# Batch 1's Z from float16 halves, and all steps from the first conversions on in another order

## The chip, the cores and the metric

One core of one Trainium2 chip runs the kernel. The core has TensorE (PE) for matrix products, VectorE (DVE), ScalarE (ACT) and GpSimd (POOL) for the rest, SyncE (SP) whose queue issues every transfer here, and 16 DMA engines. The metric is the device time of one execution in microseconds, as the median of three.

## The reference, cut to what matters

```python
def sm_attn(qq, kk, vv):
    s = scale * np.matmul(qq, kk.transpose(0, 1, 3, 2))
    s = s - np.max(s, axis=-1, keepdims=True)
    a = np.exp(s)
    a = a / (np.sum(a, axis=-1, keepdims=True) + 1e-09)
    return np.matmul(a, vv)
p_packed = sm_attn(p, k, v)                # 32 packed rows per head
out = sm_attn(q, p_packed, p_packed)       # 576 rows per head
...
h = x @ w_in                               # x: (4608, 512), w_in: (512, 1024)
sm = e / (np.sum(e, axis=-1, keepdims=True) + 1e-09)   # e = exp(h - max h)
solu = h * sm
ln = (solu - mu) / np.sqrt(var + 1e-06) * g_ln
return ln @ w_out                          # (1024, 512)
```

There are 8 batches of 8 heads, 576 rows and 64 columns per head, all float32; the weights come as float64.

## The kernel before, in words

The second attention's values are the 32 packed rows, so the kernel multiplies these by `w_in` first. For each batch b it makes Z = packed rows times `w_in` (4 heads of 32 rows side by side, 1024 columns, two groups r), and a row's h is then its attention weights a times Z. Weights a and Z are each kept as a float16 high part and a float16 low part, and a product is three float16 products.

Work per batch, each a generator whose `yield`s cut it into steps:

- `pack(b)` (steps `k0` to `k7`): k transposed (for batches 0 and 1 by PE, line 369, else by DVE, line 383), scores of the packed rows (line 399), their maximum `nmx` (DVE, 403) and exp (ACT, 406), the exps transposed by PE (422) and copied to `e1T` (424), the product with v (432), its scaling `pp` (DVE, 435), the transposed packed rows `ppT` (448), and a size (320).
- `unpack(b)` (`q0` to `q7`): q transposed, scores (504 or 516), brought back in blocks by DVE (477), maximum `mx` (481), subtraction (483), exp (486), sum (489), reciprocal (494), scaling (496), DVE's transposition (527), high part `a_h` (ACT, 530) and low part `a_l` (532).
- `make_z(b)` (`z0` to `z7`): with `ZP_BY[b]` '0' 16 float32 products of the packed rows with `w_in_sb` (570); with '1' 48 float16 products (564) of the packed rows' halves `pph` (551, 553) with the halves of `w_in`. Those halves are made by `weight_halves` (steps `H`): four times `w_hi` on ACT (342) and the low part on DVE (344), 128 by 1024 each. Z itself is split into halves by ACT and DVE (578, 580).
- `token_tile` (`t0` to `t35`, 128 rows each; every fifth one takes its rows from two batches): 12 products h = a Z (631), row maximum `nm` (DVE, 634), its scaled form and exp (ACT, 639, 652), `u` = e times h (DVE, 656), float16 halves `yhl` of u minus its mean (ACT 665, DVE 667), a transposing DMA to `yT` (670), sum of squares (ACT, 673), a row factor on POOL (676 to 683), 24 products with `w_out`'s halves `wch` and `wcl` (691) into PSUM `po` or `h`, scaling to `o_sb` (697, 699) and the DMA out (708).
- Once: the conversion of float64 weights to float32 (steps `W0` to `W3`, `O0` to `O3`: ACT 229, DVE 231, POOL or ACT 240/242, POOL 263 or 271, DVE 250), `w_out`'s halves (`C0` to `C7`, lines 305 to 313), p's transposition (`p`, 209), loads (`lp`, `lw`, `lo`, `lk`, `lq`, `lv`). Steps `Z` (lines 117, 119) and `X` (125) are products that nothing reads, made to keep PE's clock up.

Nothing schedules this at run time: the string `ORDER` of 1287 names says which generator takes its next step, and each engine runs its instructions in the order in which they are issued so. Short strings say which engine takes a step: `LOW_BY`, `PT_BY`, `KT_BY`, `QT_BY`, `E1T_BY`, `SOFT_BY`, `A2L_BY`, `SCALED_BY` ('a' ACT, 'd' DVE, 'p' or 'g' POOL).

PSUM has three two-bank tiles `h`, shared by token tiles, transposes, scores and Z, one `po` and one `pa`. A float32 tile of raw k, q or `w_out` has three buffers; `e`, `u`, `yhl` and `yT` have two each. The four `w_out` conversions work in place in the buffers of `yT` and `yhl`.

## Time and profile before

| | us |
|---|---|
| median of 3 runs | 389.76 |
| lowest and highest | 389.49, 390.90 |
| the profiled execution | 390.44 |
| its span, first to last instruction | 388.6 |
| PE busy in the span | 373.8 |
| DVE busy | 294.3 |
| ACT busy | 256.7 |
| POOL busy | 244.8 |

The profiled execution's time is 1.8 us over its span and 0.7 us over the median. The span falls into three parts. Until 54 us the weights, p, k, q and v of batch 0 arrive and are converted, and the first weights a and the first Z are made. From 54 to 364 us PE works through the products of the token tiles, with the pieces of the next batches between them. The last 21 us are the last four tiles' products with `w_out`. Rows of a timeline name an engine's work in order of time, with the idle time before it in square brackets and what ended that.

### The profile page before, as it was taken

How to read it: one execution, taken by the hardware profiler on the slowest of the kernel's cores; microseconds unless marked ns; L12 is line 12 of the kernel's file. 1: busy time of each engine (PE TensorE's matmuls, PEld its weight loads, DVE VectorE, ACT ScalarE, POOL GpSimd, SP SyncE). 2: the span in 40 equal slices, each digit the busy share in tenths (PEclk: the TensorE clock that was granted, in tenths of full speed). 3: DMA queues.
4: the chain of work that ended last, by engine and by line, in shares of the span. 5: the costliest groups of instructions: out<-in, count | busy, mean ns of one | idle time of the engine just before them, and what ended most of it. 6: DMA issues, size and time to landing. Idle time of an engine off the chain costs nothing.

```text
span 388.6 us, 8528 instructions
## 1 busy us (share of the span) xinstructions
PE 373.8 (96%) x3234; PEld 190.9 (49%) x3234; DVE 294.3 (76%) x472; ACT 256.7 (66%) x447; POOL 244.8 (63%) x410
## 2 busy tenths in 40 slices
PE   6978979999999999999999999999999999999996
PEld 6856435444545444544454455444444444444444
DVE  2577888999987987778798589977777968466631
ACT  2566799795878678955767657754658559465730
POOL 2674689887438987764555476875456658854550
PEclk9989999999999999999999999999999999999999
DMA  8999894898899999999697878873632435353561
GB/s 310 385 375 355 195 213 89 201 167 183 150 228 166 201 215 172 175 180 230 143 199 145 204 142 189 189 167 67 128 81 59 107 108 83 83 132 86 83 162 54
DMA packets 213017, 66.10 MB, mean 170 GB/s; under 512 B 192872, under 2 KB 206960, under 8 KB 212464
## 3 DMA queue, kind: packets, MB, share of 16 engines
q1 hardware_dynamic: 212976, 65.56, 74.4%
q8 instruction: 25, 0.41, 0.5%
q14 instruction: 16, 0.13, 0.1%
HBM read 37.23 MB, written 9.44 MB: 120 GB/s over the span
## 4 chain that ended last, share of the span: by engine, by line
PE 71%; DVE 4%; DMA 2%; ACT 1%; POOL 1%; issue 1%; SPq 0%; DVEq 0%; ACTq 0%
PE po L691 37%; PE h L631 19%; PE h L691 5%; PE h L564 2%; PE pa L432 2%; PE h L399 2%; PE h L516 1%; DMA yT<-yhl 1%; PE h L422 1%; DMA raw<-in_q_dram 1%; DVE u L656 1%; DVE w_in_sb L344 1%; DVE nm L634 1%; ACT e L652 1%; DVE s L477 0%
## 5 line engine op out<-in xcount | busy, mean ns | idle before, releaser
L691 PE MATMUL po<-wch,yT 128*128 128x512 f16 x512 | 160.1, 379 | 0.1
L691 PEld LDWEIGHTS <-yT 128*128 128x128 f16 x888 | 85.8, 98 | 100.6 <-issue 5.3
L691 PE MATMUL po<-wcl,yT 128*128 128x512 f16 x256 | 97.0, 379 | 0.0
L656 DVE SCALAR_TENSOR_TENSOR u<-e,s_row,h 128x1024 f32<-128x1024 f32 x36 | 45.8, 1271 | 18.3 <-ACT e L652 12.9
L667 DVE SCALAR_TENSOR_TENSOR yhl<-u,negmu,yhl 128x1024 f16<-128x1024 f32 x36 | 47.5, 1319 | 4.7 <-ACT yhl L665 4.6
L634 DVE TENSOR_REDUCE nm<-h 128x1 f32<-128x1024 f32 x36 | 43.5, 1212 | 8.3 <-PE h L631 7.9
L631 PE MATMUL h<-zh,a_h 128*128 128x512 f16 (+2 forms) x168 | 47.7, 380 | 0.7 <-ACT qT L371 0.7
L631 PE MATMUL h<-zl,a_h 128*128 128x512 f16 (+2 forms) x168 | 47.9, 380 | 0.0
L631 PEld LDWEIGHTS <-a_h 128*128 128x128 f16 (+2 forms) x336 | 27.7, 100 | 34.6 <-issue 5.2
L652 ACT ACTIVATE e<-h,nmc,z_scale 128x1024 f32<-128x1024 f32 x36 | 43.2, 1201 | 1.9 <-PE h L631 0.8
L665 ACT ACTIVATE yhl<-u,negmu 128x1024 f16<-128x1024 f32 x36 | 41.1, 1145 | 0.7
L673 ACT ACTIVATE e<-u,negmu 128x1024 f32<-128x1024 f32 x36 | 40.9, 1137 | 0.0
L639 ACT ACTIVATE nmc<-nm,z_scale 128x1 f32<-128x1 f32 x33 | 9.6, 292 | 45.9 <-DVE nm L634 45.9
L642 POOL TENSOR_SCALAR bound<-nm,z_scale 128x1 f32<-128x1 f32 x33 | 12.9, 390 | 37.6 <-DVE nm L634 36.1
L680 POOL TENSOR_SCALAR c_row<-sq,s_eps 128x1 f32<-128x1 f32 x36 | 12.8, 355 | 29.3 <-ACT e L673 26.4
L631 PE MATMUL h<-zh,a_l 128*128 128x512 f16 (+2 forms) x84 | 30.4, 379 | 0.1
L631 PE MATMUL h<-zl,a_l 128*128 128x512 f16 (+2 forms) x84 | 30.4, 379 | 0.0
L699 DVE TENSOR_SCALAR o_sb<-po,c_row,inv 128x512 f32<-128x512 f32 x18 | 14.6, 810 | 13.8 <-PE po L691 6.9
L681 POOL TENSOR_TENSOR c_row<-c_row,neg_half 128x1 f32<-128x1 f32 x36 | 22.5, 626 | 3.0
L660 ACT ACTIVATE negmu<-su 128x1 f32<-128x1 f32 x36 | 7.2, 200 | 25.5 <-DVE u L656 25.4
L496 POOL TENSOR_TENSOR a<-a,sm 128x576 f32<-128x576 f32 x16 | 20.3, 1274 | 4.9 <-DVE sm L494 4.3
L532 POOL TENSOR_TENSOR a_l<-s,a_h 128x576 f16<-128x576 f32 x14 | 20.4, 1460 | 4.5 <-ACT a_h L530 4.5
(173 smaller groups left out, 687.8 us busy)
## 6 DMA issues: line engine op xcount, KB each, us to landing
out_dram<-o_sb SPq DMA_DIRECT2D x34, 256.0 KB, 2.3
v_sb<-in_v_dram SPq DMA_DIRECT2D x8, 1024.0 KB, 8.3
raw<-in_k_dram SPq DMA_DIRECT2D x24, 288.0 KB, 4.4
raw<-in_q_dram SPq DMA_DIRECT2D x96, 72.0 KB, 2.5
zh<-in_moe_w_in_dram SPq DMA_DIRECT2D x2, 1024.0 KB, 8.0
zl<-in_moe_w_in_dram SPq DMA_DIRECT2D x2, 1024.0 KB, 7.9
raw<-in_k_dram SPq DMA_DIRECT2D x2, 1024.0 KB, 12.2
raw<-in_moe_w_out_dram SPq DMA_DIRECT2D x2, 1024.0 KB, 8.4
```

What stands on the lines that cost most here:

```text
L496: EN(nc, SOFT_BY[2 * b + 1]).tensor_tensor(out=w2, in0=w2, in1=sm.unsqueeze(2).broadcast_to([P, NB, J]), op=ALU.mult)
L532: EN(nc, A2L_BY[2 * b + r]).tensor_tensor(out=lo, in0=a2T, in1=hi, op=ALU.subtract)
L631: nc.tensor.matmul(dst_[:, cols], lhsT=lhsT, rhs=z[:, r, cols], start=bool(first), stop=bool(last))
L634: nc.vector.tensor_reduce(out=nm, in_=h, axis=AX.X, op=ALU.max, negate=True)
L652: nc.scalar.activation(e, h, AF.Exp, bias=nmc, scale=sc[:, 1:], accum_out=se)
L656: nc.vector.scalar_tensor_tensor(out=u, in0=e, scalar=s_row, in1=h, op0=ALU.mult, op1=ALU.mult, accum_out=su)
L665: nc.scalar.activation(yhl[:, 0], u, AF.Identity, bias=negmu)
L667: nc.vector.scalar_tensor_tensor(out=yhl[:, 1], in0=u, scalar=negmu, in1=yhl[:, 0], op0=ALU.add, op1=ALU.subtract)
L673: nc.scalar.activation(e, u, AF.Square, bias=negmu, accum_out=sq)
L681: nc.gpsimd.tensor_tensor(out=c_row, in0=c_row, in1=neg_half, op=ALU.pow)
L691: nc.tensor.matmul(po[:, cols], lhsT=yT[:, a, c], rhs=w[:, c, cols], start=c == 0 and t == 0, stop=c == NFC - 1 and t == 2)
L699: nc.vector.tensor_scalar(out=o_sb[:, cols], in0=po[:, cols], scalar1=c_row, scalar2=inv, op0=ALU.mult, op1=ALU.mult)
```

## The change

`ZP_BY[1]` becomes '1': batch 1's Z is made like those of batches 2 to 7, by 48 float16 products in place of 16 float32 ones, and the four pairs of `weight_halves` come before it (`H` steps moved forward). `warm_up` is cut into eleven steps: six of four float32 products, five of three wide ones. `SOFT_BY` gets an entry for each r and each of the two operations, `E1T_BY` entries for all batches, and `weight_halves` a branch for POOL that no entry takes (`HL_BY` is 'dddd'). `ORDER` is another string from its eleventh name on. Line numbers after the change are larger by 1 in the upper part of the code, by 4 from `keep_clock` on and by 8 from `z_scale` on.

```diff
-SCALED_BY = 'gggggggg'
+SCALED_BY = 'ggggggdg'
-A2L_BY = 'ddpppppppppppppp'
-SOFT_BY = 'ppppppppdppppppp'
-LOW_BY = 'appapaaa'
+A2L_BY = 'pdppppdpdpppppdp'
+SOFT_BY = 'pppppppppdppppppppdpdpppdppdpdpd'
+LOW_BY = 'aaapaaap'
-PT_BY = 'aaaa'
-KT_BY = 'ddaaaaaaaaaaaaa'
-QT_BY = 'dadaaaaaaaaaaaa'
-E1T_BY = 'aaaaaa'
+PT_BY = 'ddda'
+KT_BY = 'ddaadaaaaaaaaaa'
+QT_BY = 'dadadaaaaaaaaaa'
+E1T_BY = 'ddadaaaadddaaaaa'
-ZP_BY = '00111111'
+ZP_BY = '01111111'
+HL_BY = 'dddd'
...
     def warm_up():
-        for _ in range(24):
-            nc.tensor.matmul(spare[:, :P], lhsT=ones_f, rhs=ones_f, start=True, stop=True)
-        for _ in range(15):
-            nc.tensor.matmul(spare, lhsT=ones, rhs=ones.unsqueeze(1).broadcast_to([P, DM // P, P]), start=True, stop=True)
-        yield
+        for _ in range(6):
+            for _ in range(4):
+                nc.tensor.matmul(spare[:, :P], lhsT=ones_f, rhs=ones_f, start=True, stop=True)
+            yield
+        for _ in range(5):
+            for _ in range(3):
+                nc.tensor.matmul(spare, lhsT=ones, rhs=ones.unsqueeze(1).broadcast_to([P, DM // P, P]), start=True, stop=True)
+            yield
...
-            copy_by(nc, E1T_BY[2 * b + i0 // 8] if b < 3 else 'a')(e1T[:, i0:i0 + len(grp)], pt[:, :len(grp) * P].rearrange('p (i j) -> p i j', j=P))
+            copy_by(nc, E1T_BY[2 * b + i0 // 8])(e1T[:, i0:i0 + len(grp)], pt[:, :len(grp) * P].rearrange('p (i j) -> p i j', j=P))
...
-            EN(nc, SOFT_BY[2 * b]).tensor_tensor(out=s2[r], in0=s2[r], in1=mx.unsqueeze(2).broadcast_to([P, NB, J]), op=ALU.subtract)
+            EN(nc, SOFT_BY[4 * b + r]).tensor_tensor(out=s2[r], in0=s2[r], in1=mx.unsqueeze(2).broadcast_to([P, NB, J]), op=ALU.subtract)
...
-            EN(nc, SOFT_BY[2 * b + 1]).tensor_tensor(out=w2, in0=w2, in1=sm.unsqueeze(2).broadcast_to([P, NB, J]), op=ALU.mult)
+            EN(nc, SOFT_BY[4 * b + 2 + r]).tensor_tensor(out=w2, in0=w2, in1=sm.unsqueeze(2).broadcast_to([P, NB, J]), op=ALU.mult)
```

Three places show what the new order does. The first is PE's beginning, up to the first scores of batch 0; `ident,e` are p's transposing products, `ident,raw` the transposes of k, `ones_f` and `ones` the products that nothing reads, `kT,pT` the scores. Before:

```order
L209 MATMUL h<-ident,e 64x128 x8
L117 MATMUL po<-ones_f 128x128 x24
L119 MATMUL po<-ones 128x512 x15
L369 MATMUL h<-ident,raw 128x128 x16
L376 MATMUL h<-ident,raw 128x128 x2
L125 MATMUL po<-ones 128x384 x4
L399 MATMUL h<-kT,pT 32x288 x16
```

Now:

```order
L119 MATMUL po<-ones_f 128x128 x8
L213 MATMUL h<-ident,e 64x128 x8
L119 MATMUL po<-ones_f 128x128 x8
L377 MATMUL h<-ident,raw 128x128 x8
L119 MATMUL po<-ones_f 128x128 x8
L377 MATMUL h<-ident,raw 128x128 x8
L384 MATMUL h<-ident,raw 128x128 x2
L123 MATMUL po<-ones 128x512 x6
L407 MATMUL h<-kT,pT 32x288 x16
```

Of the 39 products that stood in one block ahead of k's transposes, 16 stand there now; 8 stand between k's transposes, 6 behind them, and 9 among what follows.

The second place is ACT around the first token tile: `e_112` is the exp of batch 1's packed scores, `qT` the copy of q's transposes of batch 1, `nmc` the first thing that ACT does for a token tile. Before:

```order
L406 ACTIVATE e_112,ssum<-h,nmx 128x2x288
L410 ACTIVATE rs<-ssum,eps_106 128x2
L305 ACTIVATE wch<-yT,gs 128x512
L371 COPY qT<-h 128x4x256
L639 ACTIVATE nmc<-nm,z_scale 128x1
L652 ACTIVATE e,se<-h,nmc,z_scale 128x1024
```

Now:

```order
L414 ACTIVATE e_112,ssum<-h,nmx 128x2x288
L309 ACTIVATE wch<-yT,gs 128x512
L418 ACTIVATE rs<-ssum,eps_106 128x2
L346 ACTIVATE w_hi<-w_in_sb,s_w 128x1024
L379 COPY qT<-h 128x4x256
L309 ACTIVATE wch<-yhl,gs 128x512
L379 COPY qT<-h 128x4x256
L647 ACTIVATE nmc<-nm,z_scale 128x1
L660 ACTIVATE e,se<-h,nmc,z_scale 128x1024
```

The first `w_hi` and a second copy of `qT` have come in between the exp and the token tile; the first of these copies stood ahead of the exp before.

The third place is DVE ahead of batch 1's Z, from the u of the third token tile on; `mx` is the maximum of batch 1's scores, `nmx` that of batch 2's packed scores. Before:

```order
L656 SCALAR_TENSOR_TENSOR u,su<-e,s_row,h 128x1024
L481 TENSOR_REDUCE mx<-s_840 128x18
L656 SCALAR_TENSOR_TENSOR u,su<-e,s_row,h 128x1024
L383 STREAM_TRANSPOSE qT<-raw 128x576
L667 SCALAR_TENSOR_TENSOR yhl<-u,negmu,yhl 128x1024
L344 SCALAR_TENSOR_TENSOR w_in_sb<-w_in_sb,s_w,w_hi 128x1024
```

Now:

```order
L664 SCALAR_TENSOR_TENSOR u,su<-e,s_row,h 128x1024
L358 TENSOR_TENSOR z_scale<-w_size,size 128x1
L359 TENSOR_SCALAR z_scale<-z_scale 128x1
L411 TENSOR_REDUCE nmx<-h 128x1
L489 TENSOR_REDUCE mx<-s_868 128x18
L664 SCALAR_TENSOR_TENSOR u,su<-e,s_row,h 128x1024
L421 RECIPROCAL rs<-rs 128x2
L557 TENSOR_SCALAR s_p<-size 128x1
L349 SCALAR_TENSOR_TENSOR w_in_sb<-w_in_sb,s_w,w_hi 128x1024
L675 SCALAR_TENSOR_TENSOR yhl<-u,negmu,yhl 128x1024
L349 SCALAR_TENSOR_TENSOR w_in_sb<-w_in_sb,s_w,w_hi 128x1024 x2
L561 SCALAR_TENSOR_TENSOR pph<-ppT,s_p,pph 128x128
```

Now three of the four low halves of `w_in` and the low half of the packed rows stand here, and the second maximum `nmx` of batch 2 has come in behind the third token tile's u.

## Rows read from the trace of the kernel before

**Rows 1.** The page: busy time of each engine in the span.

```profile
PE 373.8 (96%) x3234; PEld 190.9 (49%) x3234; DVE 294.3 (76%) x472; ACT 256.7 (66%) x447; POOL 244.8 (63%) x410
```

**Rows 2.** Busy time by stretch: length, PE, PEld, DVE, ACT, POOL, clock, DMA, GB/s.

```profile
54.00:98.00 44.00, 43.51 (x446) 20.36 (x449) 40.77 (x64) 35.69 (x65) 37.16 (x54) 1.00 0.82 160
98.00:364.00 266.00, 265.66 (x2237) 126.84 (x2227) 208.32 (x332) 179.69 (x321) 169.25 (x308) 1.00 0.72 148
364.00:385.40 21.40, 20.62 (x119) 11.20 (x117) 9.05 (x12) 7.58 (x13) 7.54 (x18) 1.00 0.55 117
```

**Rows 3.** Timeline of PE, start to first token tile: start, us, what, idle before.

```profile
4.93 7.73 PE L117 MATMUL po<-ones_f 128*128 128x128 f32 x48
...
19.71 1.21 PE L399 MATMUL h<-kT,pT 64*32 64x288 f32 x32 [0.28 <-ACT kT L378]
...
25.58 1.21 PE L422 MATMUL h<-ident,e 128*128 128x128 f32 x7 [2.28 <-ACT e L406]
...
28.63 1.67 PE L369 MATMUL h<-ident,raw 128*128 128x128 f32 x8
...
30.36 1.04 PE L369 MATMUL h<-ident,raw 128*128 128x128 f32 x8
...
32.32 0.88 PE L432 MATMUL pa<-v_sb,e1T 128*32 128x64 f32 x48 [0.32 <-DMA v_sb<-in_v_dram]
...
52.86 0.59 PE L125 MATMUL po<-ones 128*128 128x384 f32 x2
54.13 0.59 PE L631 MATMUL h<-zh,a_h 128*128 128x512 f16 x2 [0.68 <-ACT qT L371]
...
56.81 0.38 PE L631 MATMUL h<-zh,a_l 128*128 128x512 f16 x1
```

**Rows 4.** Waits of the SP queue: waiter, releaser, us in total, times, longest; its timeline.

```profile
SPq L182 <- DMA raw<-in_k_dram: 2.7, 1, 2.7
...
14.09 0.34 SPq L182 DMA_DIRECT2D g_raw<-in_moe_g_ln_dram  x1
```

**Rows 5.** The stretch behind PE's longest early wait, columns as in group 2.

```profile
28.00:30.00 2.00, 2.00 (x15) 1.67 (x12) 0.37 (x1) 0.30 (x1) 1.49 (x1) 0.53 1.15 288
```

**Rows 6.** Timeline of DVE, 33 to 90 us.

```profile
33.78 0.28 DVE L435 TENSOR_TENSOR pp<-pa,rs 128x128 f32<-128x128 f32 x1
...
43.46 0.74 DVE L481 TENSOR_REDUCE mx<-s 128x18 f32<-128x576 f32 x1
...
50.72 1.04 DVE L231 TENSOR_SCALAR yhl<-e 128x1024 int32<-128x1024 int32 x1
...
54.68 0.76 DVE L532 TENSOR_TENSOR a_l<-s,a_h 128x576 f16<-128x576 f32 x1 [0.86 <-ACT a_h L530]
...
79.88 1.29 DVE L344 SCALAR_TENSOR_TENSOR w_in_sb<-w_in_sb,s_w,w_hi 128x1024 f16<-128x1024 f32 x1
...
89.06 2.30 DVE L667 SCALAR_TENSOR_TENSOR yhl<-u,negmu,yhl 128x1024 f16<-128x1024 f32 x1
```

**Rows 7.** Timelines of ACT (first row) and POOL (second row), 77 to 93 us.

```profile
77.99 1.14 ACT L342 ACTIVATE w_hi<-w_in_sb,s_w 128x1024 f16<-128x1024 f32 x1
...
88.40 4.11 POOL L532 TENSOR_TENSOR a_l<-s,a_h 128x576 f16<-128x576 f32 x2 [0.52 <-ACT a_h L530]
```

**Rows 8.** Timeline of PE around batch 1's Z.

```profile
76.10 1.92 PE L570 MATMUL h<-w_in_sb,ppT 64*32 64x512 f32 x24
78.16 0.72 PE L399 MATMUL h<-kT,pT 64*32 64x288 f32 x16
78.67 1.06 PE L570 MATMUL h<-w_in_sb,ppT 64*32 64x512 f32 x8
79.67 0.39 PE L691 MATMUL po<-wch,yT 128*128 128x512 f16 x1
```

**Rows 9.** Chain that ended last: batch 2's Z, and the end.

```profile
146.82 1.42 PE h L564 x48
...
363.85 5.58 DMA yT<-yhl
```

More of the change, by code (lines that the diff above doesn't have):

```diff
@@ L343, in weight_halves @@
             yield
-            nc.vector.scalar_tensor_tensor(out=halves[1][g], in0=w_in_sb[:, g], scalar=s_w, in1=halves[0][g], op0=ALU.mult, op1=ALU.subtract)
+            if HL_BY[g] == 'd':
+                nc.vector.scalar_tensor_tensor(out=halves[1][g], in0=w_in_sb[:, g], scalar=s_w, in1=halves[0][g], op0=ALU.mult, op1=ALU.subtract)
+            else:
+                nc.gpsimd.tensor_scalar(out=w_in_sb[:, g], in0=w_in_sb[:, g], scalar1=s_w, scalar2=0.0, op0=ALU.mult, op1=ALU.add)
+                nc.gpsimd.tensor_tensor(out=halves[1][g], in0=w_in_sb[:, g], in1=halves[0][g], op=ALU.subtract)
             yield
```

2 lines of the change are left out of this document (1 added, 1 removed).

## The prediction

> **What bounds the kernel now.** I read the page first, then busy time by stretch, then PE's timeline and waits, then the chain that ended last. PE is busy in 374 of 389 us [rows 1], and the stretches say where the rest lies: from 54 to 98 us it lacks 0.5 us, from 98 to 364 us 0.3 us, in the last 21 us 0.8 us [rows 2]. So behind the first token tile the kernel is a row of matrix products with almost no hole. An edit there is worth what it takes out of or puts into that row, plus holes closed or opened, and these have 1.6 us to give. The other way to gain is an earlier first token product; it starts at 54.1 us, after a wait for a copy on ACT [rows 3], and tile 0 ends at about 57.0 (its last product starts at 56.8 and lasts 0.2 behind its neighbour). What leads there is a chain: batch 0's v lands at 32.3 us, which PE waits for [rows 3], `pp` follows at 33.8 on DVE, the maximum of the second half of the scores at 43.5, the last `a_l` at 54.7 to 55.4 [rows 6].
>
> **The start, up to tile 0.** In the queue of transfers only batch 0's q and one part of `w_out` change places ahead of v, so v still lands at 32.3 us. k of batch 0 lands at about 14.1, when SP's wait for it ends [rows 4]. PE used to have 24 float32 products up to there, 7.7 us of them [rows 3]; now it has 16 (5.2 us), p's transposes between (about 2) and a start at 1.2, so it is done by 8.4 to 10 and waits 4 to 6 us. A wait of 2.3 us [rows 3] was followed by a stretch at a granted clock of 0.53, which is the 1.2 GHz level, in which eight transposes took 1.67 us instead of 1.04 [rows 5, 3]. I therefore charge the low clock to k's first transposes (1.7) and to the eight products behind them: each makes two records (24 of them 48, [rows 3]), and sixteen at 0.21 us, an eighth of 1.67, are 3.4. With 1 for k's second transposes and 1.7 for the rest the first scores stand at 22 us instead of 19.7. From there DVE has some ten instructions of 0.6 to 1.2 us before `pp`, 9.5 us in all with the small ones, and gets to it at 33.4: before the earlier 33.8, because v and not the scores decides. Gain 0.3 us. This is the place where the low clock is hidden; it has about 0.3 us of cover.
>
> From `pp` on I walk DVE's queue with the durations of before. One maximum over `w_out` (1.2 us) moves behind the first half's `mx`, which comes at 40.3, but POOL stands in a 2.4 us addition and subtracts only at 41.5. The second half's `mx` comes at 43.4, as before (43.5), and it is the later half. Behind it, the second half's transposition now waits for one shift less (1.04 us, [rows 6]; it moved ahead), and the first half's `a_l` (0.76) leaves DVE for POOL. That brings the last `a_l` from 55.4 to 53.7 and the release of the PSUM tile to 53.3. POOL's `a_l` of the first half ends at 53.7 too. Tile 0 then runs without the break it has now, 2.65 us, to about 56.2.
>
> One doubt remains. POOL's `a_l` and DVE's now lie side by side; where POOL made two of them, which took 4.1 us, DVE took 2.3 us for an instruction that takes 1.3 elsewhere [rows 6, 7]. So a clash costs up to 1.0 us; the two may also miss each other, and only what lies behind 53.7 counts, so I take 0.2: tile 0 ends at 56.4 instead of 57.0. **Term: -0.6**, bounds -1.3 (first scores not late, no clash) and +1.5 (both bad). The Trainium skill, "SBUF — State Buffer", section "Who interferes with whom", says that a DVE instruction with two SBUF inputs and a GpSimd instruction that reads SBUF exclude each other for the whole instruction. By that rule, which the row at 89.06 agrees with, DVE's `a_l` would begin when POOL's ends, this term would be about -0.2 and the sum below 0.4 us higher.
>
> **What moves behind tile 0.** The second group of batch 1's q transposes stood ahead of tile 0 and now stands behind it: eight transposes, 0.95 us (1.04 with the last one's end, [rows 3]). Two products that nothing reads stand among the tiles now, 0.33 us (0.59 with the end, [rows 3]). Nothing hides PE's own work here. **Term: +1.3.**
>
> **Batch 1's Z.** From 76.10 to 79.67 us lie the float32 products with one piece of scores of 0.5 us between; 3.06 us are Z's [rows 8]. The same Z of batch 2 from float16 halves takes 1.42 us [rows 9]. **Term: -1.64.** Its cost elsewhere: four `w_hi` of 1.14 us on ACT and four low halves of 1.2 to 1.3 us on DVE [rows 7, 6] are not new, they come earlier, and `pph` comes in (0.3 and 0.4 us). DVE, busy 40.8 of 44 us between 54 and 98 [rows 2], gets some 3.3 us more to do before the sixth token tile: one low half, a share of `w_out`'s halves, `e1T` and `pph`, and small ones.
>
> **Holes among the first tiles.** I follow the bank of each PSUM tile. Before, PE lacks 0.5 us there [rows 2], of which 0.3 lies within tile 0. Now: (a) behind tile 0 the exps' transposes need the bank that the first `qT` copy frees, and on ACT `w_hi` stands ahead of that copy: 0.5 us; (b) tile 1 needs the second copy's bank: 0.3; (c) two scores and the next packed scores between tiles 2 and 3 follow each other through two banks that DVE clears: 0.3; (d) batch 2's exps are transposed ahead of tile 1's products with `w_out`, and the second exp waits for `nmx`, which now stands behind the third tile's u on DVE: 0.7. Together 1.8, of which I take 1.2, since (b) and (c) vanish if DVE runs 0.3 us ahead. Against the 0.2 us that are there outside tile 0, **Term: +1.0**, bounds -0.2 and +3. In the walk Z's own halves are ready at 84.5 and PE arrives at 86.2, so the new wait costs nothing with 1.7 us of cover.
>
> **98 to 364 us.** The same products in another order; DVE is at 78%, ACT and POOL at 68 and 64% [rows 2]. A fourth to a half of the subtractions and scalings of the scores go from POOL to DVE. There are 0.3 us of holes to win, and new ones can open. **Term: 0**, bounds -0.3 and +1.2.
>
> **The end.** The chain waits from 363.9 to 369.4 for a transposing DMA, and PE loses 0.8 us in the stretch [rows 9, 2]. Now the products with `w_out` of tiles 32 to 35 stand in a row behind tile 35's own, 20.7 us. Counted back from their end, tile 33's `yT` is issued at -20.0 and is needed at -15.6, those of 34 and 35 can be issued when a `yT` buffer is free, 5.2 us ahead of need. If a DMA takes as long as that one did, 5.6 us, 0.4 to 1 us is lost; at the usual 3.9 nothing. **Term: -0.7**, bounds -0.8 and +0.6.
>
> **Sum.** -0.6 + 1.3 - 1.64 + 1.0 + 0 - 0.7 = -0.6 us, on the profiled execution from 390.4 to 389.8 (its span of 388.6 and 1.8 around it). The median of the runs lies 0.7 us below that execution, so on it the sum is 389.76 - 0.6 = **389.2 us**. A measurement of this kernel can tell 0.5%, 1.95 us, from no change. So I forecast no change that counts.
>
> **Rivals.** *Faster: the early holes don't open.* My walk rounds each instruction up by some 0.05 us, and the 60 on DVE between tile 0 and batch 1's Z make 3 us of that, more than all four holes. For it speaks that PE lost only 0.5 us there with DVE 93% busy [rows 2]; against it, that holes (a) and (d) come from an order on one engine and not from its load. Price: that term falls to its bound of -0.2 and tile 0 ends at 55.8: -1.2 and -0.6 more, 387.4. It decides where DVE is 0.7 us ahead of my walk. Chance 0.27.
>
> *Slower: the start slips.* The low clock behind the wait for k lasts until batch 0's exps are transposed. The products and transposes between take twice as long, the scores come at 23.5, and DVE reaches `pp` 2 us after v instead of 1. From there on nothing absorbs it, since the chain to tile 0 is one queue: each us later at `pp` is one at the end. It decides as soon as the first scores are later than 22.3 us. For it: behind the wait of 2.3 us the clock was still low in the eight transposes at 28.6 us [rows 3, 5], and the new wait is twice as long. Against it: the next eight, at 30.4 us, ran at full rate [rows 3]. Price +2 to 3.5 us on the sum, 392.2 in the middle. Chance 0.18.
>
> *The change doesn't do what it says.* Three low halves stand on DVE straight ahead of Z. If each takes 2.3 instead of 1.3 us, as the DVE row at 89.06 did beside POOL's work [rows 6, 7], they end 3 us later, 1.4 us beyond the cover, and the gain of 1.64 us is gone. Time 390.7, within no change. Chance 0.10. It decides where two of the three clash.
>
> **How the numbers follow.** The forecast has 0.45, with its own range 387.9 to 391.2; with the third rival 0.55 for no change. The first rival gives faster 0.27, the second slower 0.18. The range reaches into both until about 0.1 is left out on each side: past 387.4 to 386.6, where the moved transposes would be the only loss left, and to the second rival's middle, 392.2.
>
> **What would show it.** In the timeline of after: PE idle from about 9 to 14 us and the granted clock 0.5 behind it; first scores near 22 us; `pp` at 33.4 on DVE, tile 0's products from 53.5 without a break; Z's 48 products in 1.42 us with no wait for `w_in_sb` or `pph`; waits of PE for `qT` and for the exp between 56 and 80 us of 1 to 2 us together; at the end no wait of PE for `yT` over 0.4 us. Wrong would be the whole if tile 0 ended before 55 or after 58 us, or if the stretch from 100 to 364 us lost more than 1.5 us.

## The result and the profile after the change

The changed kernel takes 394.17 us (median of four runs, 393.45 to 394.93) beside 389.84 us of the kernel before: 1.0107 times as long, interval 1.0075 to 1.0139. Measured once more beside three of the experiments it took 393.43 us, 1.0062 times the time before (1.0042 to 1.0082). It is slower by 2.3 to 4.3 us, beyond the end of the forecast range (392.2). Its profiled execution took 393.5 us; the span is 391.7 us against 388.6. Its ten single executions lie between 392.5 and 394.9 us; one stretch of low clock, shown below, occurs in about half of them and explains only a part of that spread.

The page's line of busy times, to be held against [rows 1]:

```profile
PE 373.2 (95%) x3250; PEld 190.7 (49%) x3250; DVE 305.2 (78%) x493; ACT 254.1 (65%) x438; POOL 228.0 (58%) x400
```

TensorE has 0.6 us less to do and the span is 3.1 us longer. The same cut by stretch, first before, from tile 0's end on (length, PE, PEld, DVE, ACT, POOL, clock, DMA, GB/s):

```profile
57.03:98.00 40.97, 40.74 (x435) 19.29 (x437) 38.63 (x61) 32.70 (x58) 34.85 (x51) 1.00 0.80 160
...
364.00:385.25 21.25, 20.62 (x119) 11.20 (x117) 8.94 (x11) 7.58 (x13) 7.54 (x18) 1.00 0.55 116
57.03:385.25 328.22, 327.01 (x2774) 157.33 (x2772) 255.88 (x402) 219.97 (x391) 211.63 (x377) 1.00 0.71 147
385.25:388.60 3.35, 0.00 (x1) 0.00 (x0) 0.54 (x1) 0.00 (x0) 0.00 (x0) 0.95 0.15 53
```

And after:

```profile
57.16:98.00 40.84, 39.32 (x471) 19.94 (x470) 38.23 (x64) 33.16 (x58) 29.09 (x43) 1.00 0.83 174
98.00:200.00 102.00, 101.60 (x886) 48.37 (x885) 86.64 (x146) 73.95 (x137) 64.70 (x128) 1.00 0.93 184
200.00:364.00 164.00, 163.96 (x1317) 77.17 (x1316) 128.74 (x196) 104.77 (x184) 94.62 (x179) 1.00 0.55 122
364.00:387.85 23.85, 23.15 (x131) 12.51 (x128) 10.24 (x13) 7.69 (x13) 6.99 (x18) 1.00 0.51 127
57.16:387.85 330.69, 328.03 (x2800) 157.99 (x2798) 263.85 (x416) 219.57 (x389) 195.40 (x368) 1.00 0.70 148
387.85:391.70 3.85, 0.00 (x0) 0.00 (x0) 0.55 (x1) 0.00 (x0) 0.00 (x0) 1.00 0.11 36
```

Length less PE is idle time. Tile 0 ends 0.13 us later (57.16 for 57.03). From there to 98 us idle time grows from 0.23 to 1.52, from 98 to 364 us from 0.34 [rows 2] to 0.44, from 364 us to the last product from 0.63 to 0.70; behind the last product 3.35 become 3.85. Busy time grows by 1.0. Together 3.1 us. The growth in busy time is partly waiting too: a product's modelled end lies 0.16 us behind the start of its successor and covers a wait of that size; counted from starts, 0.7 of it are waits.

TensorE's timeline of after, up to tile 0 (start, us, what, idle before), to be held against [rows 3]:

```profile
14.26 1.97 PE L377 MATMUL h<-ident,raw 128*128 128x128 f32 x8 [6.71 <-DMA raw<-in_k_dram]
...
21.17 1.20 PE L407 MATMUL h<-kT,pT 64*32 64x288 f32 x32
...
43.01 0.39 PE L281 MATMUL pa<-ssq,ones_f 128*128 128x8 f32 x2 [1.26 <-DVE ssq L290]
43.32 2.35 PE L578 MATMUL h<-w_in_sb,ppT 64*32 64x512 f32 x16
45.60 1.97 PE L377 MATMUL h<-ident,raw 128*128 128x128 f32 x8
...
54.57 0.59 PE L639 MATMUL h<-zh,a_h 128*128 128x512 f16 x2
```

The low clock behind the wait for k is there as forecast (transposes of 1.97 us at 14.3). A second one was not: eight transposes take 1.97 us again at 45.6. By the windows the granted clock was 0.50, the 1.2 GHz level, from 10.85 to 17.67 and from 44.98 to 51.81 us:

```profile
10.85:17.67 6.82, 3.42 (x16) 3.42 (x17) 4.85 (x5) 4.78 (x5) 4.67 (x3) 0.50 1.08 393
44.98:51.81 6.83, 5.73 (x34) 3.35 (x31) 4.36 (x11) 5.11 (x10) 5.17 (x4) 0.50 0.93 149
```

The rows of the first tiles and of the end that wait, and batch 1's Z (to be held against [rows 8]):

```profile
65.11 0.33 PE L446 MATMUL pa<-ident,pp 128*128 128x128 f32 x1 [0.41 <-DVE pp L443]
...
70.25 0.72 PE L407 MATMUL h<-kT,pT 64*32 64x288 f32 x16 [0.50 <-DVE s L485]
...
80.35 1.11 PE L430 MATMUL h<-ident,e 128*128 128x128 f32 x7 [0.41 <-ACT e L414]
...
88.04 0.41 PE L572 MATMUL h<-w_hi,pph 64*32 64x512 f16 x8
...
89.46 0.39 PE L699 MATMUL po<-wch,yT 128*128 128x512 f16 x1
...
100.84 0.39 PE L699 MATMUL po<-wch,yT 128*128 128x512 f16 x1 [0.40 <-DMA yT<-yhl]
...
385.06 0.27 PE L699 MATMUL h<-wch,yT 128*128 128x256 f16 x1 [0.69 <-DVE o_sb L707]
```

Z takes 1.42 us (88.04 to 89.46) and waits for nothing. The others are the holes of the new order, and the last one is a wait that the kernel before did not have.

### The profile page after: what moved, and what is told of

Read it like the earlier page. It is cut to its first block, busy times and chain, and to the rows that moved or that the text cites. A ratio compares the mean times of both kernels' runs of the same rounds, so it can differ in the third digit from the quotient of the medians.

```text
span 391.7 us, 8521 instructions
## 1 busy us (share of the span) xinstructions
PE 373.2 (95%) x3250; PEld 190.7 (49%) x3250; DVE 305.2 (78%) x493; ACT 254.1 (65%) x438; POOL 228.0 (58%) x400
## 4 chain that ended last, share of the span: by engine, by line
PE 83%; DMA 8%; ACT 3%; DVE 2%; POOL 1%; issue 1%; SPq 0%; DVEq 0%; POOLq 0%
PE po L699 41%; PE h L639 22%; PE h L699 5%; DMA v_sb<-in_v_dram 3%; PE h L572 3%; PE pa L440 3%; DMA zh<-in_moe_w_in_dram 2%; DMA zl<-in_moe_w_in_dram 2%; PE h L524 2%; PE h L407 2%; PE h L430 1%; ACT wch L309 1%; DMA yT<-yhl 1%; PE h L578 1%; ACT e L414 1%
## 5 line engine op out<-in xcount | busy, mean ns | idle before, releaser
L650 POOL TENSOR_SCALAR bound<-nm,z_scale 128x1 f32<-128x1 f32 x33 | 14.6, 443 | 58.7 <-DVE nm L642 57.1
L689 POOL TENSOR_TENSOR c_row<-c_row,neg_half 128x1 f32<-128x1 f32 x36 | 21.3, 591 | 3.0
L688 POOL TENSOR_SCALAR c_row<-sq,s_eps 128x1 f32<-128x1 f32 x36 | 11.4, 318 | 19.4 <-ACT e L681 16.2
L639 PEld LDWEIGHTS <-a_l 128*128 128x128 f16 (+2 forms) x168 | 14.3, 100 | 16.8
L540 POOL TENSOR_TENSOR a_l<-s,a_h 128x576 f16<-128x576 f32 x12 | 17.2, 1433 | 8.9 <-ACT a_h L538 8.8
L414 ACT ACTIVATE e<-h,nmx 128x576 f32<-128x576 f32 x16 | 12.0, 748 | 15.1 <-DVE nmx L411 13.0
```

Source lines behind the costliest of these rows:

```text
L414: nc.scalar.activation(dst, both if by_rows else both.rearrange('p n (a t) -> p n a t', t=32), AF.Exp, bias=nmx, accum_out=ssum[:, r:r + 1])
L540: EN(nc, A2L_BY[2 * b + r]).tensor_tensor(out=lo, in0=a2T, in1=hi, op=ALU.subtract)
L639: nc.tensor.matmul(dst_[:, cols], lhsT=lhsT, rhs=z[:, r, cols], start=bool(first), stop=bool(last))
L650: by.tensor_scalar(out=bound, in0=nm, scalar1=-1.0 / U_MAX, scalar2=sc[:, :1], op0=ALU.mult, op1=ALU.max)
L689: nc.gpsimd.tensor_tensor(out=c_row, in0=c_row, in1=neg_half, op=ALU.pow)
```

## The experiments

Theory after the first look: three places lose, each by itself, the stretch of low clock ahead of tile 0, hand-overs among the first tiles (SP's queue among them), and the last tile. Rivals: VectorE's load sets the pace, so a mended hole only moves; or the low halves that came forward do it. In the diffs a name with a number is one step of `ORDER`, counted from 0, and only the parts that matter are shown. Five runs leave out part of the computation: e9_lows and e12_zlows the low halves of `w_in`, e15_znone, e16_none and e17_zplace both halves. The table gives each run's time as a ratio to the kernel before beside it, and from its profiled execution the start of tile 0's first product and the span (us).

| run | ratio, interval | tile 0 | span |
|---|---|---|---|
| before | 1 | 54.13 | 388.6 |
| after | 1.0107 (1.0075 to 1.0139) | 54.57 | 391.7 |
| after_again | 1.0062 (1.0042 to 1.0082) | 53.08 | 390.7 |
| e1_fill | 1.0083 (1.0059 to 1.0108) | 54.46 | 391.6 |
| e2_warm | 1.0122 (1.0100 to 1.0145) | 55.74 | 393.0 |
| e6_zsplit | 1.0064 (1.0040 to 1.0088) | 52.41 | 391.3 |
| e3_tail | 1.0077 (1.0050 to 1.0103) | 54.24 | 393.5 |
| e5_holes | 1.0074 (1.0051 to 1.0097) | 54.88 | 392.5 |
| e7_yT | 1.0156 (1.0127 to 1.0185) | 55.83 | 394.7 |
| e9_lows | 1.0103 (1.0084 to 1.0121) | 53.93 | 392.5 |
| e16_none | 1.0083 (1.0047 to 1.0119) | 53.12 | 391.2 |
| e8_zonly | 1.0077 (1.0058 to 1.0096) | 54.67 | 393.9 |
| e12_zlows | 1.0039 (1.0022 to 1.0057) | 53.85 | 390.2 |
| e15_znone | 1.0008 (0.9983 to 1.0032) | 54.31 | 389.6 |
| e17_zplace | 1.0066 (1.0044 to 1.0088) | 53.42 | 391.7 |
| e10_z32 | 1.0238 (1.0213 to 1.0263) | 53.90 | 397.4 |
| e11_best | 1.0174 (1.0151 to 1.0197) | 52.02 | 396.4 |
| e13_mend | 1.0024 (1.0001 to 1.0047) | 52.76 | 388.8 |
| e14_mend2 | 1.0002 (0.9971 to 1.0034) | 52.94 | 389.7 |
| e18_exp | 1.0020 (0.9995 to 1.0045) | 52.72 | 389.0 |

**The low clock ahead of tile 0.**

```diff
 e1_fill
-X:4 O3:1 g:0 k1:0 g:1 S:0
+X:4 g:0 g:1 O3:1 k1:0 X:5 X:6 S:0
 e2_warm
+Z:2 Z:3 Z:4 Z:5 Z:6 Z:7 Z:8
 k0:0
 e6_zsplit
-z0:1 z0:2 q0:14 O3:0 z0:3 z0:4 z0:5 lk1:0 lk2:0 X:3 X:4 O3:1 g:0 k1:0 g:1 S:0 k1:1
+z0:1 X:3 lk1:0 k1:0 g:0 q0:14 O3:0 z0:2 z0:3 z0:4 O3:1 g:1 k1:1 z0:5 lk2:0 X:4 X:5 S:0
...
-z0:6 z0:7 z0:8 k1:2
+z0:6 z0:7 k1:2 z0:8 X:6
```

> The changed kernel with four of the products that nothing reads moved from 49 to 53 us to the place where TensorE waits 1.26 us for ssq (41.7 to 43.0), and g_sb's copy one place earlier on ScalarE so that they need not wait for it. All that is computed is the same. Theory A: the granted clock of 0.5 from 45.0 to 51.8 us comes from how little TensorE did just before it, and it costs the start of the token tiles 1 us (k's eight transposes take 1.97 instead of 1.06, ScalarE's copy of them holds up the sum of the second half, POOL's scaling and so tile 0). Then the clock stays at 1.0 there, the transposes take 1.1 us, sm's wait of 1.45 us on VectorE falls under 0.5, tile 0's last product starts near 55.9 instead of 56.94, and the time falls by 0.8 to 1.2 us, to about 393.0 (median of the changed kernel 394.17). Rival B: the low stretch is a late answer to the wait of 6.7 us for k, whatever stands at 42 us: then it stays, and the time stays within 0.3 us of 394.2. Rival C: the clock stays up, but tile 0 has another chain (POOL's a_l behind its neighbour) and starts no earlier: time within 0.3 us as well, with the low stretch gone.

> The changed kernel with seven of the eleven steps of the products that nothing reads put back in one block ahead of k's transposes (16 float32 ones and nine wide ones there), as before the change. Prediction's claim: the low clock behind the wait for k is hidden, since v's landing at 32 us and not the scores decides pp. Then the clock stays at 1.0 from 10 to 18 us, the first scores come at 18.8 to 20 instead of 21.2, and pp is still at 33.0; tile 0 and the whole time move by less than 0.3 us, except where the three wide products that no longer stand at 34 us bring the later low stretch forward or lengthen it (up to 1 us slower). Rival B (the later low stretch answers the wait for k): it disappears here, tile 0 comes 1 us earlier, the time is 393.0.

> The changed kernel once more, with nothing edited, as the yardstick beside the three others on the same chip. Its four times so far lie at 393.5 and 394.9 us, and the first four edits gave 391.8 to 396.0. Theory: the single times differ by which stretches of low clock one execution gets (TensorE waits for yT at 101 us for 0.4 us here, for 1.8 us in the execution of e3_tail, and only there a further stretch at 0.5 follows, from 102.9 to 106.3 us, and po's products come 2.5 us later). Then the times spread over 391.9 to 395 us again, median 393.5 to 394.5. Rival: the changed kernel has one time, 394.2 within 0.8 us, and the edits e3_tail and e5_holes (392.4) are worth the whole difference.

> The changed kernel with batch 0's Z made in four blocks of four float32 products again instead of two blocks of eight, with k's transposes and the products that nothing reads between them: in before four such blocks took 1.0 us each, in the changed kernel two blocks of twice the size take 1.0 us each at full clock, so TensorE had 2 us less to do between 38 and 45 us and fell to 0.5 from 45.0 to 51.8. All that is computed is the same. Theory A (low clock answers how much TensorE did from 38 to 45 us): no stretch at 0.5 begins between 40 and 54 us; k's second transposes take 1.1 instead of 1.97 us, ScalarE's copy of them no longer holds up sm (wait of 1.45 us on VectorE under 0.6), tile 0's first product starts at 53.0 to 53.7 instead of 54.57, the time is 0.8 to 1.5 us shorter than the changed kernel's beside it. Rival B: tile 0 hangs on VectorE's and POOL's a_l and not on the clock: the stretch goes, but tile 0 starts at 54.3 or later and the time stays within 0.3 us. Rival C: the stretch stays although TensorE has no wait over 0.4 us from 38 to 45 us.

e2_warm has no low clock before 44 us, its scores come at 19.1, and `pp` stands at 32.6 on VectorE, 0.4 us earlier than in after (32.96): but for these 0.4 us the first stretch is hidden, as the prediction said. Its late stretch stays and is longer (44.4 to 54.6), so the wait for k is not its cause. In e1_fill the wait for `ssq` fell to 0.56 us and the stretch came all the same (46.1 to 53.0), with 6.44 us of work from 38 to 45 us: Theory A as put there missed. after_again, the same kernel, shows an execution without it. The same two stretches of time in after, after_again and e6_zsplit, and of before, one fence each:

```profile
38.00:45.00 7.00, 5.74 (x64) 2.80 (x63) 6.41 (x19) 3.98 (x7) 4.72 (x4) 1.00 0.85 217
45.00:52.00 7.00, 5.90 (x35) 3.54 (x32) 4.53 (x12) 5.28 (x10) 5.34 (x4) 0.51 0.93 148
```
```profile
38.00:45.00 7.00, 5.74 (x62) 2.92 (x65) 6.44 (x18) 3.87 (x6) 4.46 (x3) 1.00 0.91 229
45.00:52.00 7.00, 5.59 (x61) 3.13 (x54) 6.21 (x16) 6.51 (x12) 6.37 (x6) 1.00 0.86 138
```
```profile
38.00:45.00 7.00, 6.76 (x63) 3.57 (x52) 6.41 (x19) 4.41 (x7) 4.98 (x4) 1.00 0.83 207
45.00:52.00 7.00, 5.73 (x61) 2.84 (x59) 6.25 (x15) 6.75 (x13) 6.43 (x5) 1.00 1.01 161
```
```profile
38.00:45.00 7.00, 6.66 (x62) 3.19 (x46) 6.76 (x20) 4.17 (x6) 4.27 (x3) 1.00 0.84 215
45.00:52.00 7.00, 5.47 (x61) 2.60 (x59) 6.18 (x15) 6.69 (x13) 4.68 (x6) 1.00 1.05 175
```

The changed kernel leaves TensorE 5.74 us of work from 38 to 45 us where before had 6.66, and then falls to the lower level in one execution and not in the other. By the mean granted clock five of its ten measured executions are like the first (0.981 to 0.983), five like the second (0.987 to 0.991). With Z in four blocks and the work back (6.76) none of e6_zsplit's eight and e13_mend's twelve is under 0.987, nor is any of the thirty of e11_best, e14_mend2 and e18_exp, which have the same edit. Whether the amount of work or its arrangement does it was not separated: e1_fill had 6.44 us with Z in its two blocks and fell. What the stretch costs is read from the two executions of one kernel: tile 0's first product at 54.57 or 53.08, 1.5 us; in this pair 1.0 of that reaches the end of the span. Over the ten executions the price is less clear: the five with the stretch have a median of 393.6 us, the five without it 393.2, and the two groups overlap. The path is the one that the chain to tile 0 takes through ScalarE, here in VectorE's timeline of after (first fence) and of after_again (second):

```profile
46.67 0.74 DVE L497 TENSOR_REDUCE sm<-a 128x18 f32<-128x576 f32 x1
48.86 0.27 DVE L502 RECIPROCAL sm<-sm 128x18 f32<-128x18 f32 x1 [1.45 <-ACT sm L499]
```
```profile
47.02 0.74 DVE L497 TENSOR_REDUCE sm<-a 128x18 f32<-128x576 f32 x1
48.14 0.27 DVE L502 RECIPROCAL sm<-sm 128x18 f32<-128x18 f32 x1 [0.38 <-ACT sm L499]
```

ScalarE's copy of `kT` stands ahead of `sm` in its queue and waits for the slow transposes. The Trainium skill, "TensorE: Matmul & The Clock Gate", section "What's actually happening", says that the count of slow products at a kernel's start differs between runs of one kernel. That a stretch in the middle of a busy kernel can differ so too is what these two executions show.

e6_zsplit gained 0.7 us more at tile 0 than after_again and ended 0.6 us later; its median, 393.01 us beside 393.43, misses the 0.8 to 1.5 us that were expected. Its rows of SP and TensorE around tile 3's transposing DMA say where it went:

```profile
91.27 4.81 SPq L163 DMA_DIRECT2D raw<-in_q_dram  x8
96.19 1.70 SPq L678 DMA_TRANSPOSE yT<-yhl  x1
...
100.24 0.39 PE L699 MATMUL po<-wch,yT 128*128 128x512 f16 x1 [1.60 <-DMA yT<-yhl]
```

`yhl` was ready at 93.9, but eight loads of q stood ahead on SP's queue until 96.1.

**SP's queue and the early hand-overs.**

```diff
 e7_yT
-lq3:2 k2:17
...
-z1:7 lq3:3
+lv3:0 lq3:2 lq3:3
 e5_holes
-H:1 C4:1 t0:0 t0:1 q1:1 C6:0 q1:2 C3:2 q1:3
+C4:1 t0:0 t0:1 q1:1 C6:0 q1:2 C3:2 q1:3 H:1
-k1:20 t0:7 H:2 C5:2 t2:0
+t0:7 H:2 C5:2 t2:0 k1:20
+k1:23
 k2:4
-k2:11 t2:7 H:6 H:7 H:8 t1:11
+t2:7 H:6 H:7 H:8 t1:11 k2:11
```

> The changed kernel with eight of the loads of batch 3's q moved on SP's queue from ahead of tile 3's transposing DMA to behind v's load. In the changed kernel sixteen issues of 0.55 to 0.75 us each stand between two transposing DMAs (84.7 and 97.1 us), in before fourteen, then a DMA, then eight. Theory: SP's queue and not the tile's halves sets when yT is issued; then it is issued by 96 us, TensorE's wait for yT at 100.8 us (0.4 us in the changed kernel's profile, 0.5 to 0.6 in three others, 1.8 in that of e3_tail) is gone in every execution, and with it the stretch of low clock that followed it there: 0.4 us less where the wait was short, 2 to 2.5 us less where it was long, median 0.5 to 1.2 us below the changed kernel's beside it, and times no longer above 394 us. Rival: yT is late because the tile's low half is (VectorE is 94% busy): the DMA starts no more than 0.3 us earlier and nothing changes.

> The changed kernel with four steps moved, all between tile 0 and batch 1's Z: the first w_hi on ScalarE behind the two copies of qT (wait of 0.24 us ahead of tile 1); tile 2's first half between batch 1's pp and its transposing product (0.41 us); the product of total ahead of batch 2's scores (0.50 us for s); the transposes of batch 2's exps one quarter of tile 1's w_out products later (0.55 us for e). Theory: these four holes are TensorE's own and nothing else is late next, so 0.9 to 1.4 us go: 393.0. Rival: VectorE, 94% busy in this stretch, is what sets the pace, and the holes move on to other instructions: TensorE's idle time from 57 to 98 us stays over 1.2 us, and the time stays within 0.4 us of 394.2.

In e7_yT the DMA left as soon as `yhl` was there and the wait at 100.8 us was gone, but the loads then stood ahead of the next transposing DMA, where TensorE waited 2.38 us at 114.5: the jam moved by one tile. Its profiled execution also had a late stretch of low clock, 44.2 to 54.4 us, so its time is not the price of the loads alone. (In before, too, sixteen loads stand ahead of tile 3's DMA, and not fourteen as the expectation says.) In e5_holes the waits of TensorE (in total, times, longest) became these:

```profile
PE po L699 <- ACT o_sb L705: 1.2, 1, 1.2
...
PE h L512 <- DVE u L664: 0.4, 1, 0.4
PE pa L440 <- ACT e1T L432: 0.4, 1, 0.4
...
PE h L512 <- DVE ppT L456: 0.2, 1, 0.2
```

The four holes closed and these took their place, the first by an edit of mine: the products that were put ahead of the transposes need the bank that ScalarE's `o_sb` frees, and that copy stands behind the exp. The rival was right that holes move; whether VectorE's load is why was asked next.

```diff
 e9_lows, e12_zlows
-out=halves[1][g], in0=w_in_sb[:, g], scalar=s_w, in1=halves[0][g]
+out=low[g][:, :32], in0=w_in_sb[:, g, :32], scalar=s_w, in1=halves[0][g][:, :32]
 e15_znone, e16_none, e17_zplace: besides
-nc.scalar.activation(halves[0][g], w_in_sb[:, g], AF.Copy, scale=s_w)
+nc.scalar.activation(high[g][:, :32], w_in_sb[:, g, :32], AF.Copy, scale=s_w)
```

> The changed kernel with the four low halves of w_in computed on 32 of 1024 columns each, and Z's products of the second kind reading the high halves in their place (this leaves out part of the computation: the low parts of w_in, in all Z from halves). It takes some 4.6 us off VectorE between 60 and 88 us and nothing off TensorE or ScalarE. Theory A: the holes among the first tiles (waits for pp, s, e and yT, 2 us together between 57 and 112 us) exist because VectorE, 94% busy, runs late, and the low halves that came forward are what makes it late: then the waits fall under 1 us and the time is 1 to 2 us below the changed kernel's (393.4 to 394.2), about 392. Rival B: each hole is a hand-over within one short order on one engine, or SP's queue ahead of yT, and VectorE's load has nothing to do with it: waits within 0.4 us of 2 us, time within 0.5 us of 393.5.

> The same omission in the changed kernel: both halves of w_in made on 32 of 1024 columns, w_out's halves read in their place (this leaves out w_in in the Z of batches 1 to 7). e9_lows, without the low halves alone, gained nothing (394.2). Theory: in the changed kernel the halves stand where they cost nothing, and its holes are hand-overs of the new order: within 0.7 us of the changed kernel (393.4 to 394.2). Rival: ScalarE's four w_hi are what makes the copies and exps late: 1 to 2.5 us below it.

Neither gained anything outside the changed kernel's own spread. The waits stayed (`pp`, `s`, `e`, and 0.9 and 1.6 us for `yT`). So in the changed order neither half of `w_in` is what opens the holes, nor are the 4.6 us of VectorE's load that e9_lows takes away; what ends the waits in the rows are hand-overs between neighbours on their queues.

**Z from float16 alone.**

```diff
 e8_zonly, on the kernel before; H:1 to H:8 stand behind k1:14, t0:7, t1:4, q1:9, q1:11, t1:7, t1:9, t2:5
-ZP_BY = '00111111'
+ZP_BY = '01111111'
-z1:3 k2:7 t3:5 t1:10 z1:4 q1:17
+k2:7 t3:5 t1:10 q1:17
...
+z1:3 z1:4
 q1:21
 e17_zplace
+z1:3 z1:4
 t1:11
 e10_z32, on the changed kernel; H:1 to H:8 behind q1:22, q1:25, k2:18, t3:9, q2:1, t5:1, t4:6, t4:9
-ZP_BY = '01111111'
+ZP_BY = '00111111'
+z1:1
 z1:2
```

> The kernel before with one part of the change alone: batch 1's Z from float16 halves. The eight steps of w_in's halves are moved forward (from among batch 2's first steps to between tile 0 and tile 2's yhl), and Z's products 1.5 steps of tile 1 later; the rest of the order, the engines' shares and the warming products are those of before. Prediction's term: 1.64 us less TensorE work for Z (1.42 instead of 3.06). If that holds and the cover that the prediction named is there, 388.2 (390.0 - 1.6 + 0.2). Rival: w_hi and the low halves, 4.6 us on ScalarE and 5 us on VectorE, which is 93% busy from 54 to 98 us, stand ahead of tiles 1 to 3 and open holes of 1 to 3 us: 389.5 to 391.5, and Z then waits for w_in's low halves or the tiles for u and yhl.

> e8_zonly (the kernel before with batch 1's Z from float16 halves) with the four low halves of w_in computed on 32 of 1024 columns each and Z's products of the second kind reading the high halves (this leaves out the low parts of w_in). e8_zonly took 394.1 beside 391.1 of before; its waits for yT (1.7 us at 81.4, 2.0 at 104) follow a first yhl that VectorE finishes behind the low halves. Theory A: VectorE's 5 us are the price; without them the waits for yT ahead of 85 us go, and the time falls to 390 to 391.5. Rival B: ScalarE's four w_hi are, or SP's queue: time within 1 us of e8_zonly's.

> e8_zonly (the kernel before with batch 1's Z from float16 halves) with both halves of w_in made on 32 of 1024 columns only, on ScalarE and VectorE, and Z's products of batches 1 to 7 reading w_out's halves in their place (this leaves out w_in in those Z; the number and size of the products stay). e8_zonly was 3.0 us slower than before, e12_zlows, without the low halves alone, 1.5 to 1.9 us slower. Theory: the halves' work ahead of the early tiles is the whole price and Z's products save what the prediction took for them: 1.0 to 1.7 us below the kernel before. Rival: the price lies in where Z's products and batch 2's first steps now stand: still 1 us or more above before.

> e15_znone with Z's float16 products back at the place where the float32 ones stood in before, straight ahead of tile 1's first product with w_out (both halves of w_in made on 32 columns, w_out's halves read in their place, as there). In before the float32 products, 76.1 to 79.67 us, lay over the transposing DMA of tile 1, issued at 74.85 with 3.6 us to its landing at 78.45, 1.2 us ahead of need; in e15_znone, where 1.5 steps of tile 1 come first, TensorE waits 1.79 us there. Theory (Z's long products were the cover of that DMA): with 1.42 us of products in place the wait is 0.2 to 0.6 us, and the time is 0.7 to 1.5 us below the kernel before. Rival: the time stays at that of e15_znone (1.0008 of before), since whatever Z saves the next transposing DMA takes.

> The changed kernel with batch 1's Z from float32 again, its sixteen products in two blocks of eight, and the eight steps of w_in's halves put back among batch 2's first steps: the new order without the new Z. By the prediction's term the products cost 1.64 us more (3.06 instead of 1.42); by the two blocks of eight of batch 0 in the changed kernel, 1.0 us each, only 0.6 more. Theory A (the halves cost the early tiles as much as Z saves): ScalarE loses 4.6 and VectorE 5 us of work ahead of Z, waits between 57 and 112 us fall by 1 us or more, and the time is 0.3 to 1.0 us below the changed kernel's, 392.5 to 393.5. Rival B: the new order's holes have nothing to do with the halves; the time is 0.6 to 1.6 us above, 394.2 to 395.5.

In the order of before the same part costs 3.0 us. The low halves on VectorE are 1.5 us of that (1.0077 to 1.0039), the high ones on ScalarE 1.2 (to 1.0008), and even with neither the time is that of before and not 1.64 us under it. In e15_znone TensorE waits at tile 1's first product with `w_out`:

```profile
79.53 0.39 PE L694 MATMUL po<-wch,yT 128*128 128x512 f16 x1 [1.79 <-ACT pph L554]
```

The profile names `pph`, which ended at the same moment; but the product reads `yT`, whose DMA was issued at 75.77 and took 3.7 us to land, 79.5 too, and in e12_zlows and e8_zonly the same product's 1.7 us are put down to `yT`. In before Z's float32 products lay there, 76.10 to 79.67 us [rows 8], while that DMA was on its way (issued at 74.85, 3.6 us to landing). So, as these traces read, they were its cover; the run that was to test this could not. With the shorter products put back there, e17_zplace, both expectations missed, for a third reason, TensorE's rows:

```profile
78.65 0.63 PE L567 MATMUL h<-wch,pph 64*32 64x512 f16 x16 [1.80 <-ACT pph L554]
80.72 1.91 PE L567 MATMUL h<-wch,pph 64*32 64x512 f16 x32 [1.45 <-DVE pph L556]
```

The float32 products read `ppT` as it is; the float16 ones need it split, on ScalarE behind a `yhl` and on VectorE behind that. Behind these waits TensorE ran at a granted clock of 0.50 from 79.8 to 86.6 us, which is in this run's time as well. The changed kernel puts Z 12 us later, where the split is long done, and pays with nothing there. e10_z32 was a poor experiment: the halves' steps, put among batch 2's, held up what follows (waits of 1.89 us for `z_scale` at 108.1 and 0.97 for `squares`), so its time says nothing about Z. It shows one thing: two blocks of eight float32 products take 1.09 us each, 2.2 in all, where before needed 3.06.

**The end, and all mended together.**

```diff
 e3_tail
-t34:14 t34:15 t34:16 t35:11 t35:12 t35:13 t33:15 t33:16 t35:14 t35:15
+t33:15 t33:16 t35:11 t35:12 t35:13 t34:14 t34:15 t34:16 t35:14 t35:15
 e13_mend: the edits of e6_zsplit and e3_tail, and
-z1:7 lq3:3
+t3:8 lq3:3
 e14_mend2: besides, those of e5_holes without k2:11
 e18_exp: besides
-t3:2 t0:11 t0:12 C7:1 t2:4 t3:3
+k2:7 k2:8 t3:2 t0:11 t0:12 C7:1 t2:4 t3:3 k2:9
```

> The changed kernel with the last six products with w_out of tile 34 put back between the two halves of tile 35's own, and tile 33's o_sb and output ahead of them. Theory: the wait of TensorE for o_sb at the end (0.69 us) is cover that the new order took away; it goes, and o_sb of tile 33 no longer holds up that of tile 35 on VectorE. Expected 0.7 us less, 393.5, up to 1.0 less if the last outputs also leave earlier. Rival: the end is set by the last outputs' transfers, which queue up on SP, and the gain of 0.7 us on TensorE does not reach the end: 394.2 within 0.3.

> e10_z32 with, besides, batch 0's Z in four blocks (as in e6_zsplit, which had no late stretch of low clock and tile 0's first product at 52.4 us), the tail of e3_tail, and four of batch 3's q loads moved on SP's queue behind tile 3's transposing DMA. All that is computed is as in the kernel before. If the four gains add (tile 0 1.1 us earlier, end 0.7, yT 0.4 to 1.6, and what e10_z32 gives), 390.5 to 391.5; if what is gained at tile 0 is given back at the transposing DMA of 97 us, as in e6_zsplit, 392 to 393.

> The changed kernel with the edits of e6_zsplit (batch 0's Z in four blocks, no late stretch of low clock) and e3_tail together, and four of batch 3's q loads moved on SP's queue behind tile 3's transposing DMA. Everything is computed. Theory (the losses sit at three named places and add up): e6_zsplit's profiled execution, 393.1 us, less its wait of 1.6 us for yT at 100 us, less the 0.85 us of the end: 390.6, within 0.3% of the kernel before. Rival: what is won at one place is given back at the next, as e6_zsplit gave back what it had won at tile 0: 392 to 393.

> e13_mend and three of the steps of e5_holes: the first w_hi on ScalarE behind the two copies of qT, tile 2's first half between pp and its transposing product, total's product ahead of batch 2's scores. Theory: the three holes of 0.4 to 0.5 us each are orders on one queue and close: 1 to 1.4 us below e13_mend. Rival: TensorE only comes earlier to the next copy (in e5_holes it waited 0.4 us for u, 0.4 for e1T and 0.2 for ppT in their place): within 0.4 us of e13_mend.

> e14_mend2 with batch 2's second packed scores one product block earlier on TensorE, their maximum ahead of tile 3's on VectorE and their exp ahead of tile 2's negmu on ScalarE, against the last of the early holes (0.53 us for e at 78.6 us there). Theory: the hole closes and nothing else opens: 0.3 to 0.6 us below e14_mend2 (1.0002 of before), 0.9985 to 0.9995. Rival: tile 2's yhl comes 0.7 us later and its transposing DMA is late instead: 1.000 to 1.003.

In e3_tail's chain that ended last tile 34's products lie between the halves of tile 35 and no wait is left (start, us, what):

```profile
383.09 2.62 PE h L699 x24
385.71 1.29 PE po L699 x6
387.00 2.63 PE h L699 x24
```

Its time (1.0077 of before) shows no gain by itself. Its profiled execution is long for another reason: a wait of 1.8 us for `yT` near 101 us and one more stretch of low clock behind it, 102.9 to 106.3. e11_best carried e10_z32's fault and says nothing more. e13_mend's profiled execution came out as the sum that was expected (390.57 us for 390.6; span 388.8 against 388.6 of before). Its median is 391.93 us, 1.0024 of before: by the ratios 1.5 us below after_again and 3.2 below after. All its twelve executions (390.57 to 392.46) lie below all ten of the changed kernel (392.53 to 394.93). In e14_mend2 and e18_exp each further hole closed, and waits for `u`, `e1T`, `o_sb` and `yT` of 0.2 to 0.6 us came in; neither can be told from before or from e13_mend. No version that computes everything beat the kernel before.

## Why the prediction was wrong

**Wrong is the sum: three terms, the start, the holes and the end, missed the same way at once.** The predicted -0.6 became +3.1 on the profiled execution. From tile 0's end to the last product TensorE has the same products as before but for those that the terms name, worth -0.4 us (0.95 + 0.33 - 1.64), and yet that stretch is 2.5 us longer (328.22 to 330.69): waits and hand-overs grew by 2.8 us, where the terms had +0.3 (1.0, 0 and -0.7).

- *The start, term -0.6.* Right up to `pp`: k waited 6.7 us, the low clock followed, the first scores came at 21.2 (forecast 22), `pp` at 32.96 (33.4), and e2_warm shows that this stretch is hidden. Failed at the walk from `pp` on: it took durations at full clock for granted. With the second stretch tile 0 ends 0.13 us later than before, without it 1.4 us earlier (55.66, at the bound of -1.3). The wait for `ssq` and Z in two dense blocks could have been seen in the order: both take work from TensorE ahead of 45 us.
- *The clash of the two a_l* did not happen in after: POOL's ran from 52.66 to 53.95, VectorE's from 54.49 in 0.75 us, because the second stretch had made it late. In after_again and the eight other profiled executions of the new order without that stretch it did happen, and VectorE's took 1.3 to 1.4 us (rows in the last section). The rule of the Trainium skill, "SBUF — State Buffer", section "Who interferes with whom", by which such a pair excludes each other, agrees with these rows. It cost nothing at tile 0, whose products ran without a break in after_again (53.08 to 55.66). A `yhl` of 2.18 us at 82.41 beside POOL's subtractions, like the 2.30 of [rows 6], agrees with it too.
- *What moves behind tile 0, +1.3:* the transposes took 1.16 us (57.16 to 58.32), the two spare products 0.63, some 0.2 of each in hand-overs. Slightly low.
- *Z, -1.64:* right as a term (1.42 us, no wait), and the cover of the halves was right for the new order (e9_lows, e16_none). It is no price of the part by itself, as e8_zonly shows; there, as the traces read, the cover goes and is worth more than Z.
- *Holes, +1.0:* idle time from tile 0's end to the end of batch 2's Z grew from 0.35 (57.03 to 109.51 us) to 1.92 (57.16 to 111.37), so by 1.6; counted from starts it is some 1.8. Cases (a), (c) and (d) came as described, 0.3 to 0.7 us each, and (b) with 0.24. Missed: batch 1's transposing product behind `pp` (0.41 us), and SP's queue. There sixteen loads stand ahead of tile 3's DMA, as before, but they begin 4.0 us later (86.63 for 82.67), behind tile 2's DMA, while TensorE gets to tile 3 only 2.1 us later (100.44 for 98.39): a wait of 0.4 us in after, 0.6 in after_again and 1.8 in e3_tail. That queue was not walked for the tiles.
- *98 to 364 us, 0:* +0.1 by idle time. Right.
- *The end, -0.7:* failed. The wait for `yT` is gone, as said, but I walked the transfers alone. Tile 35's halves share a bank, and the six products that hid the copy between them (1.29 us) had moved away: 0.69 us, which is gone in e3_tail's trace. Behind the last product 0.5 us more pass, with SP's closing instructions; every kernel of the new order has that, and its cause stays open.
- *The rivals.* The slower one had the sign, its price and the low clock, but not the place: its condition, scores later than 22.3 us, was not met. Low clock came from later work, in some executions only, so that its price fits is luck (and the middle of its +2 to 3.5 us on 389.2 is 392.0, not 392.2). The faster one fell with the holes, which opened. That Z would wait for clashing low halves did not happen.

e13_mend bears the reading out: Z's blocks spread, the tail's products back and four loads moved take away 1.5 to 3.2 us with everything else as it is. It shows the three together; e6_zsplit and e3_tail alone gained nothing in time (1.0064 and 1.0077 beside 1.0062), so the price of each place is read from traces. That the rest, some 1 us, is hand-overs that can only be moved, e14_mend2 and e18_exp suggest but do not show.

## What to carry to other kernels

Products that look too long may be the cover of a transfer or the work that keeps the clock up: before they are shortened or packed more densely, look for what lands under them and what the engine then does until its next wait. When an order is rewritten, walk every queue past the moved step, SP's among them, and every bank at the last tile. A saving on the engine that bounds is bought where its preparation runs, and a part whose preparation costs nothing in one order can cost almost twice its gain in another.
